# A spectral adaLN block on one core: scattered partition order of the frequencies, filter halves loaded in place, head and join reordered

## The chip, the cores and the metric

The kernel runs on one core of a Trainium2 chip. The metric is the device time of one launch in microseconds (us). Engines are named as in the profile: PE does matrix multiplications, PEld loads their weights, DVE and ACT do elementwise work and read PSUM, POOL does elementwise work in SBUF, and SP issues most transfers.

## The reference

One adaLN block on x of 2048 rows by 640 columns, in bfloat16. The rows are normalised, scaled and shifted by a modulation of `c`, filtered in the frequency domain by a complex filter W of 2048 by 321, and added back with a gate; then follow a second normalisation and a gated MLP of width 1728.

```python
sa, ca, ga, sb, cb, gb = six parts of silu(c) @ w_mod
h = _layernorm(x) * (1 + ca) + sa
x = x + ga * irfft2(rfft2(h) * (w_r + 1j * w_i))
h = _layernorm(x) * (1 + cb) + sb
x = x + gb * ((silu(h @ w_gate) * (h @ w_up)) @ w_down)
```

## The kernel before, in words

The whole schedule is written out by hand: the order of the calls in the source is the order of the instructions on each engine, and each SP transfer waits for the landing of the SP or ACT transfer eight places earlier, as the built program has it.

**Head (to about 35 us).** The row index of x is split as 1024 h + 8 p + t. For each of eight t, `st_a` (L368) multiplies two normalised tiles with a table of cosines and sines over the partitions and leaves 127 frequencies kap = p + 1 on the partitions, and one column for the two special rows; `ht_ev` (L371) copies that out, `st_b` (L377, L379) transforms the 640 columns with `Rs`, the table `Rp` scaled by 1 + ca, and `a_ev` (L383) writes A. Statistics of the rows come from `bn` on DVE (L328, L329) or `act_stats` on ACT (L333, L334), the power from POOL (L343), and `xhat` (L353 on DVE, L355 on POOL) normalises. `idle_pe` (L310) and `idle2` (L361) are matrix multiplications on a tile of ones whose results nobody reads.

**The filter.** `Wt` holds, for every partition (a frequency kap up to 128), 16 blocks of 321 columns of W: blocks 0 to 7 are rows kap + 256 k, blocks 8 to 15 are rows 255 - p + 256 k, that is, in falling order over the partitions. The first half is loaded directly (`load_w`, L284); the second is copied from DRAM to DRAM in reversed order (`flip`, L280) and then read back (L477). `wsum` (L388) adds the imaginary and the real part into a third plane.

**Join (35 to 66 us).** A is transposed so that a column l lies on the partitions of its 128 entries: `t2_dma` (L511) does four groups of columns by DMA transposes, `t2_pe` (L533) the first ones on PE. Then, for 21 groups g of up to four columns: `mix` (L552) on PE, `prod` (L576) on DVE multiplying with Wt, `stage_b` (L583), a copy on ACT (L586), `stage_c` (L608) and a copy (L617) into Em and Er. The special rows have a path of their own: `sp_w` (L406, L408) prepares their filter, `sp_sa` and `sp_sums` (L393, L415) their shift, `sp_gather` (L626) collects them from all four transposes on POOL, and `sp_mm` (L635, L640, L644) and `sp_ev` (L654, L659, L662) treat them at the groups of `SPG`; two small transfers (L663, L664) put them into row 127 of Em and Er. `ga_mod` (L669) and `mod_col` (L565) compute parts of the modulation from parts of w_mod (L478, L524, L525).

**After that.** A loop over 16 tiles (L1217 to L1222) makes x1, and the MLP (L924 to L1149) follows. Their weights are issued on SP behind the join's transfers (L766 to L778).

Of the kernel before, what the change touches and what calls it, by code (L numbers as in the profile page):

```python
# [87 lines left out]
def _tables():  # L88
# [12 lines left out]
    kap = p + 1  # L101
    M = np.zeros((P, 8, 2, 2, 128))
    H = np.zeros((128, 8, 2, P))
    for t in range(8):
        a = 2.0 * np.pi * ((kap[None, :] * (8 * p[:, None] + t)) % S) / S
        for h in range(2):
            b = 2.0 * np.pi * ((kap[None, :] * (1024 * h + 8 * p[:, None] + t)) % S) / S
            M[:, t, h, 0], M[:, t, h, 1] = np.cos(b), -np.sin(b)
        M[:, t, :, 0, 127], M[:, t, :, 1, 127] = 1.0, ((-1.0) ** p)[:, None]
        H[:, t, 0], H[:, t, 1] = np.cos(a.T), np.sin(a.T)  # L110
        H[127, t, 0], H[127, t, 1] = 1.0, (-1.0) ** p
# [9 lines left out]
    T["Ks"] = np.concatenate([K[:, 1], np.where((p % 2 == 0) & (p < 127), -1.0, 1.0)[:, None], np.zeros((128, 1))], 1).astype(_NPBF)  # L121
# [45 lines left out]
def adaln_block_kernel(ctx, tc, A_x, A_w_r, A_w_i, B_x, B_w_gate, B_w_up, B_w_down, c, w_mod, out):  # L167
# [37 lines left out]
    identb = const.tile([P, 128], BF16, name="identb")  # L205
    mv = const.tile([P, NT, 2], F32, name="mv")
# [32 lines left out]
    Wrev = rE.cut(18464, [2, 322], parts=16)  # L239
# [21 lines left out]

    nc.scalar.dma_start(c_row[:], c)
    wmca_v = wm_v[:, :, D:2 * D]
# [4 lines left out]
    load_x(2)  # L268
    nc.sync.dma_start(wm_ca[:, 0:3], wmca_v[:, 0:3])
    nc.sync.dma_start(wm_ca[:, 3:5], wmca_v[:, 3:5])  # L270
    load_m(1, 3)
    nc.sync.dma_start(Rp[:], R_dram)
    load_x(3)
    load_m(3, 8)

    dram = ctx.enter_context(tc.tile_pool(name="dram", bufs=1, space=bass.MemoryType.DRAM))
    Wflip = [dram.tile([P, 8, 321], BF16, name=n) for n in ("wflip_i", "wflip_r")]

    def flip(w, f):
        nc.sync.dma_start(f[:].rearrange("p k l -> k p l"),  # L280
                            bass.AP(tensor=w.tensor, offset=w.offset + 255 * 321, ap=[[256 * 321, 8], [-321, P], [1, 321]]))

    def load_w(i, w):
        nc.sync.dma_start(Wt[:, i, 0:8, :], bass.AP(tensor=w.tensor, offset=w.offset + 321, ap=[[321, P], [256 * 321, 8], [1, 321]]))  # L284
# [7 lines left out]
    for i, w in ((0, A_w_i), (1, A_w_r)):  # L292
        nc.sync.dma_start(Wrow[:, i, :], w.rearrange("(k2 k1) l -> k2 k1 l", k1=P)[:, 0, :])  # L293
    nc.sync.dma_start(Ktab[:], K_dram)

# [8 lines left out]
    nc.gpsimd.memset(SL[:], 0.0)  # L304
    nc.vector.tensor_reduce(out=mask4[:], in_=identb[:].rearrange("p (m r) -> p r m", r=4), axis=mybir.AxisListType.X, op=ALU.add)
# [19 lines left out]
    if True:  # L325
        def bn(ti):
            for k in range(2):
                nc.vector.bn_stats(bn6a[:, ti % 2, k, :], x_sb[:, ti, 320 * k:320 * k + 320])  # L328
            nc.vector.bn_aggr(mv[:, ti, :], bn6a[:, ti % 2])  # L329
# [15 lines left out]
        def xpair(lo):  # L345
            nc.vector.scalar_tensor_tensor(nmean[:, lo:lo + 2], mv[:, lo:lo + 2, 0], -1.0, rstd[:, lo:lo + 2], ALU.mult, ALU.mult)
            xhat(lo, nc.gpsimd)
            xhat(lo + 1, nc.vector if lo in (4, 6, 14) else nc.gpsimd)
# [41 lines left out]
        def sp_sa():  # L390
            mps = psum[:, 5, 448:448 + NC5]
            mod_cols(mps, wm_sa)
            nc.vector.tensor_copy(sa_col[:], mps)  # L393
# [17 lines left out]
        def sp_sums():  # L411
            sps = psum[:, 3, 384:384 + NL]
            for i in range(10):
                r, c2 = i // 2, i % 2
                nc.tensor.matmul(sps, lhsT=SL[:, r, c2, :], rhs=Rp[:, r, 81 * c2:81 * c2 + 81], start=(i == 0), stop=(i == 9))  # L415
            nc.vector.tensor_scalar_mul(SA[:], sps, 256.0)

# [3 lines left out]
        idle_pe(4)  # L421
        nc.scalar.activation(sc_f[:], cps, ACT.Silu)
        act_stats(3)
        nc.gpsimd.tensor_copy(sc_rep[:], sc_f[:].unsqueeze(2).to_broadcast([P, NC5, 128]))
        bn(0)
        bn(1)
        rstd_of(0, 2)
        nc.vector.tensor_copy(sc_col[:], sc_f[:])
        bn(2)
        xhat(0, nc.vector)  # L430
        xhat(1, nc.vector)
        act_var(3)
        rstd_of(2, 2)
        act_stats(5)
        bn(4)
        nc.vector.scalar_tensor_tensor(nmean[:, 2:4], mv[:, 2:4, 0], -1.0, rstd[:, 2:4], ALU.mult, ALU.mult)
        xhat(3, nc.gpsimd)
        xhat(2, nc.vector)
        idle_pe(3)
        idle2(9)  # L440
        st_a(0)
        ht_ev(0)
        act_var(5)
        rstd_of(4, 2)
        mps = psum[:, 3, 32:32 + 32 * NC5]
# [3 lines left out]
        nc.vector.tensor_scalar_add(one_p_ca[:], mps, 1.0)  # L449
        nc.vector.tensor_scalar_mul(sa4[:], mask4[:], one_p_ca[:, 4:5])  # L450
        nc.vector.tensor_scalar_mul(Rs[:, 1, 0, :], Rp[:, 4, :], sa4[:, 0:1])
        nc.scalar.mul(Rs[:, 0, 0, :], Rp[:, 0, :], one_p_ca[:, 0:1])
        nc.vector.tensor_scalar_mul(Rs[:, 1, 1, :], Rp[:, 4, :], sa4[:, 1:2])
        nc.vector.tensor_scalar_mul(Rs[:, 1, 2, :], Rp[:, 4, :], sa4[:, 2:3])
        nc.scalar.mul(Rs[:, 0, 1, :], Rp[:, 1, :], one_p_ca[:, 1:2])
        nc.vector.tensor_scalar_mul(Rs[:, 1, 3, :], Rp[:, 4, :], sa4[:, 3:4])
        nc.vector.tensor_scalar_mul(Rs[:, 0, 2, :], Rp[:, 2, :], one_p_ca[:, 2:3])
        nc.scalar.mul(Rs[:, 0, 3, :], Rp[:, 3, :], one_p_ca[:, 3:4])
        on_dve = {(4, 1), (5, 1), (6, 1)}
        for t in range(8):  # L460
            if t + 1 < 8:
                idle2(6 if t == 0 else 1)
# [4 lines left out]
            u = 2 * t + 6  # L467
            if u < NT:
                bn(u)
            if u - 2 < NT:  # L470
                xpair(u - 2)
            if u < NT:
                bn(u + 1)
                rstd_of(u, 2)
                if t == 0:
                    for i in range(2):
                        nc.sync.dma_start(Wt[:, 2 * i, 8:16, :], Wflip[i][:])  # L477
                    nc.sync.dma_start(wm_r[:, :, 0, :], wm_m[:, :, 0, :])  # L478
            if t == 6:
                nc.gpsimd.dma_start(wm_sa[:], wm_v[:, :, 0:D])  # L480
                nc.gpsimd.tensor_copy(Wrev[:, :, 0:321], _rev(Wrow, 320, [[321, 2], [-1, 321]]))
            if t == 7:
                sp_w()
# [8 lines left out]
            if t == 6:  # L492
                wsum(48, 64, 0, nc.vector)
# [10 lines left out]
    if True:  # L504
# [41 lines left out]
        def mix(g):  # L546
            ls = groups[g]
            n = len(ls)
            xps = banks(6 if g == 2 else 2 + 2 * (g % 2), 2, [4, 256])
            for i, l in enumerate(ls):  # L550
                B2, j = B2of[l][0:2]
                nc.tensor.matmul(xps[:, i, 0:192], lhsT=B2[:, j, :], rhs=KS2, start=True, stop=True)  # L552
                if i == 0:
                    for c5 in {NG - 3: (0, 1), NG - 2: range(NC5), NG - 1: (2, 3, 4)}.get(g, ()):
                        mod_col(psum[:, 2 + 2 * (g % 2), 192 + c5:193 + c5], wm_r[:, :, 1 + g % 2], c5)
# [22 lines left out]
        def stage_b(g, PP):  # L578
            n = len(groups[g])
            yps = banks((g + 1) % 2, 1, [4, 128])  # L580
            for ps in (1, 0):
                for i in range(n):
                    nc.tensor.matmul(yps[:, i, :], lhsT=_rev(PP, 64 * n * ps + i, [[n, 128]]), rhs=identb[:],  # L583
# [40 lines left out]
        def sp_gather():  # L624
            for B2, n, ls in spec:
                nc.gpsimd.tensor_tensor(B2sp[:, ls], B2[:, 0:n, 127], SA[:, ls], ALU.add)  # L626
# [4 lines left out]
        def sp_mm(i, g):  # L631
            b = 2 + 2 * (g % 2)
            if i == 0:
# [16 lines left out]
        def sp_ev(i, g):  # L650
            b = 2 + 2 * (g % 2)
            if i == 0:
# [47 lines left out]
        SPG = (10, 12, 14)  # L700
# [3 lines left out]
        xps0 = mix(0)  # L704
        prod(0, xps0, 0)
        prod(0, xps0, 1)
        t2_pe(2)
        xps1 = mix(1)
        prod(1, xps1, 0)
        prod(1, xps1, 1)  # L710
# [13 lines left out]
        wsum(0, 16, 8, nc.vector)  # L724
# [630 lines left out]
```

## Time and profile before

| What | Value |
|---|---|
| Runs | 253.07, 254.86, 255.16 us; median 254.86 |
| Profiled execution | 253.12 us, span 251.3 us |
| Granted TensorE clock | 0.999 |
| DVE and ACT busy | 81% and 66% of the span |
| Transfers | 32.50 MB, HBM read 24.80 MB, written 3.94 MB |
| First x tile's statistics | 3.03 us |
| Last `st_b` ends | 34.54 us |
| First `prod` | 37.45 us |
| First s1em (end of the join) | 66.19 us |

The span runs from the first instruction to the last; the time of the execution has 1.8 us more around it. A row of a timeline gives start, duration, engine, line, operation, result and operands, and in brackets how long the engine stood idle before it and what it then waited for. A row of the windows gives the time of the stretch, busy time of each engine in it, granted clock, mean share of the 16 DMA engines in use and what they moved in GB/s. SPq is SP's queue of transfer issues.

### The profile page before, as it was taken

How to read it: one execution, taken by the hardware profiler on the slowest of the kernel's cores; microseconds unless marked ns; L12 is line 12 of the kernel's file. 1: busy time of each engine (PE TensorE's matmuls, PEld its weight loads, DVE VectorE, ACT ScalarE, POOL GpSimd, SP SyncE). 2: the span in 40 equal slices, each digit the busy share in tenths (PEclk: the TensorE clock that was granted, in tenths of full speed). 3: DMA queues.
4: the chain of work that ended last, by engine and by line, in shares of the span. 5: the costliest groups of instructions: out<-in, count | busy, mean ns of one | idle time of the engine just before them, and what ended most of it. 6: DMA issues, size and time to landing. Idle time of an engine off the chain costs nothing.

```text
span 251.3 us, 5925 instructions
## 1 busy us (share of the span) xinstructions
PE 237.8 (95%) x2237; PEld 185.9 (74%) x2237; DVE 204.5 (81%) x497; ACT 166.5 (66%) x327; POOL 70.1 (28%) x102
## 2 busy tenths in 40 slices
PE   8598976999999999999999999999999999999994
PEld 3476755988899888778887778888775566556773
DVE  4898567996579999688999996878998788779974
ACT  2887743879789788768865388776247777774220
POOL 5348611599070715002002320000442000003410
PEclk9999999999999999999999999999999999999999
DMA  5987999999999899900002310400511000000111
GB/s 150 384 277 155 286 385 213 178 349 367 232 362 284 233 264 176 195 28 4 0 3 53 80 50 29 49 7 4 104 52 55 0 0 0 4 0 1 55 52 52
DMA packets 42766, 32.50 MB, mean 129 GB/s; under 512 B 21473, under 2 KB 39378, under 8 KB 42738
## 3 DMA queue, kind: packets, MB, share of 16 engines
q1 hardware_dynamic: 40976, 26.99, 41.4%
q0 software_dynamic: 1616, 5.10, 8.5%
q8 instruction: 17, 0.28, 0.5%
q14 instruction: 11, 0.09, 0.1%
q10 hardware_dynamic: 146, 0.04, 0.1%
HBM read 24.80 MB, written 3.94 MB: 114 GB/s over the span
## 4 chain that ended last, share of the span: by engine, by line
PE 77%; DMA 11%; SPq 9%; ACT 1%; issue 1%; DVE 0%; DVEq 0%; ACTq 0%
PE psum L1076 36%; PE psum L947 19%; DMA rM<-in_w_mod_dram 8%; PE psum L1046 6%; PE psum L924 3%; SPq L284 3%; PE psum L685 3%; DMA rE<-tab_M 3%; SPq L280 2%; PE psum L1217 2%; PE psum L1220 2%; PE psum L1034 2%; PE psum L583 1%; SPq L293 1%; PE psum L608 1%; PE psum L565 1%
## 5 line engine op out<-in xcount | busy, mean ns | idle before, releaser
L1076 PEld LDWEIGHTS <-rW 128*128 128x128 bf16 (+1 forms) x429 | 41.9, 98 | 12.7
L1076 PE MATMUL psum<-rW 128*128 128x256 bf16 (+1 forms) x247 | 42.2, 287 | 0.0
L973 POOL TENSOR_TENSOR rM<-rM,rL 128x320 f32<-128x320 f32 x6 | 5.4, 906 | 96.7 <-ACT rL L972 96.7
L947 PEld LDWEIGHTS <-rE 128*128 128x128 f16 (+1 forms) x196 | 19.0, 97 | 7.8
L576 DVE TENSOR_TENSOR rM<-psum,rW 128x384 bf16<-128x384 f32 (+2 forms) x42 | 20.4, 543 | 3.3 <-PE psum L552 1.9
L947 PE MATMUL psum<-rE 128*128 128x320 f16 (+1 forms) x147 | 22.9, 299 | 0.0
L1107 ACT COPY rH<-psum 128x384 f32<-128x384 f32 (+2 forms) x27 | 13.9, 517 | 7.3 <-PE psum L1076 5.6
L1076 PEld LDWEIGHTS <-rE 128*128 128x128 f16 x156 | 15.3, 98 | 4.8
L1114 ACT COPY rX<-psum 128x384 f32<-128x384 f32 (+2 forms) x27 | 14.0, 519 | 7.1 <-PE psum L1076 6.9
L1111 DVE TENSOR_TENSOR rH<-psum,rM 128x512 bf16<-128x512 f32 (+1 forms) x24 | 15.0, 623 | 4.4 <-PE psum L1076 2.6
L1130 ACT ACTIVATE rL<-psum 128x384 bf16<-128x384 f32 (+2 forms) x27 | 14.4, 532 | 5.6 <-PE psum L1076 3.4
L1115 DVE TENSOR_TENSOR rX<-psum,rX 128x384 f32<-128x384 f32 (+2 forms) x27 | 16.3, 603 | 1.9 <-ACT rX L1114 1.6
L1222 DVE SCALAR_TENSOR_TENSOR rM<-psum,rX 128x640 f32<-128x640 f32 x16 | 13.0, 820 | 4.3 <-ACT rL L689 2.9
L1101 ACT COPY rM<-psum 128x384 f32<-128x384 f32 (+2 forms) x27 | 13.9, 515 | 4.0 <-PE psum L1076 3.9
L1076 PE MATMUL psum<-rW,rE 128*128 128x256 bf16 (+1 forms) x78 | 15.6, 290 | 0.0
L1076 PE MATMUL psum<-rE,rY 128*128 128x256 f16 (+1 forms) x78 | 15.6, 290 | 0.0
L1131 ACT ACTIVATE rL<-rX 128x384 bf16<-128x384 f32 (+2 forms) x27 | 15.1, 558 | 0.0
L328 DVE BATCH_NORM_STATS2 bn6a<-rX 128x6 f32<-128x320 bf16 x28 | 12.3, 479 | 3.0 <-DMA rX<-in_A_x_dram 3.0
L1046 PE MATMUL psum<-rW 128*128 128x256 bf16 x130 | 14.5, 273 | 0.0
L586 ACT CAST rY<-psum 128x512 bf16<-128x512 f32 (+2 forms) x21 | 12.0, 579 | 3.2 <-PE psum L583 2.9
L916 DVE TENSOR_TENSOR rA<-psum,rM 128x320 bf16<-128x320 f32 (+1 forms) x27 | 12.1, 470 | 2.4 <-PE psum L924 2.3
L1046 PEld LDWEIGHTS <-rW 128*128 128x128 bf16 x130 | 12.7, 98 | 1.6
(230 smaller groups left out, 624.8 us busy)
## 6 DMA issues: line engine op xcount, KB each, us to landing
out_dram<-rA SPq DMA_DIRECT2D x31, 80.0 KB, 1.6
rX<-in_A_x_dram SPq DMA_DIRECT2D x7, 320.0 KB, 7.3
rA<-in_B_w_down_dram SPq DMA_DIRECT2D x2, 960.0 KB, 15.3
rY<-in_B_w_gate_dram POOLq DMA_DIRECT2D x2, 832.0 KB, 7.7
rM<-in_w_mod_dram SPq DMA_DIRECT2D x2, 800.0 KB, 11.2
rM<-in_w_mod_dram SPq DMA_DIRECT2D x1, 1600.0 KB
rW<-in_B_w_gate_dram SPq DMA_DIRECT2D x1, 1440.0 KB, 10.0
rW<-in_B_w_up_dram SPq DMA_DIRECT2D x2, 640.0 KB, 7.2
```

Of the source, the lines that this page charges most:

```text
L576: nc.vector.tensor_tensor(PPs[g][:, v0:v1, hl], xv[:, v0:v1, hl], in1, ALU.mult)
L947: nc.tensor.matmul(o, lhsT=lhs[rows(k), k], rhs=rhs[rows(k), k], start=start and k == ks[0], stop=stop and k == ks[-1], skip_group_check=True)
L1046: nc.tensor.matmul(gu[u], lhsT=Wgu[:, u, c5, ff * 128:(ff + 1) * 128], rhs=h2T[:, :, c5, :], start=(c5 == 0), stop=(c5 == NC5 - 1))
L1076: nc.tensor.matmul(o[:, f], lhsT=w, rhs=b, start=(start and f == 0 and i == 0), stop=(stop and f == len(groups[g]) - 1 and i == len(ops) - ...
L1101: nc.scalar.copy(c0, X)
L1107: nc.scalar.copy(c2, X)
L1111: nc.vector.tensor_tensor(c11, Z, c0, ALU.add)
L1114: nc.scalar.copy(c3, X)
L1115: nc.vector.tensor_tensor(c22, Y, c3, ALU.add)
L1130: nc.scalar.activation(g21, X, ACT.Silu, scale=-1.0)
L1131: nc.scalar.activation(g22, c22, ACT.Silu, scale=-1.0)
L1222: nc.vector.scalar_tensor_tensor(x1[:, t, :].rearrange("p (m r) -> p m r", r=4), ops.rearrange("p r m -> p m r"), 1.0, x_sb[:, t, :].rearr ...
```

## The change

The frequencies get another order over the partitions: kap = 16 (p // 16) + 16 - p % 16, falling within each block of 16 partitions and rising from block to block, with the special column at partition 112. With it both halves of Wt can be read with plain steps: the upper one with eight transfers per plane (all partitions, one block each), the lower one with eight per plane (16 partitions, eight blocks each). A permuted identity, identx, swaps partitions 112 and 127 in `stage_b`, so that the special row is at 127 again behind it. Beside this, orders change:

- wm_ca's load goes ahead of the third pair of x tiles; Rp is split over ACT's queue and SP's; the w_mod part for ga and the one for sa (`wm_sa`, before on POOL's queue) are issued on SP, the first between the two halves of the filter, the second behind them.
- Statistics of tile 1 go from DVE to ACT, those of tile 5 from ACT to DVE; the scaling of Rs goes to ACT and POOL; `xhat` of the odd tiles goes to DVE; fillers change.
- `sp_w` goes behind the last `st_b`; the sums of the filter for columns 48 to 63 (first half) and 0 to 15 go to POOL; `sp_sums` becomes `sp_mm(3)` at g 5, the other three steps go from g 10, 12, 14 to 9, 11, 13; the w_mod product for sa goes into `mix(3)`; both ga_mod go ahead of `mix(2)`.
- The transfers of row 127 into Em and Er go from POOL's queue to SP's.

```diff
-    kap = p + 1
+    kap = 16 * (np.arange(P) // 16) + 16 - np.arange(P) % 16
+    kin = kap.copy()
+    kap[112] = 113
...
+    def load_up(i, w):
+        for j in range(8):
+            nc.sync.dma_start(Wt[:, 2 * i, j, :], bass.AP(tensor=w.tensor, offset=w.offset + (16 + 256 * j) * 321,
+                                                         ap=[[16 * 321, 8], [-321, 16], [1, 321]]))
+
+    def load_down(i, w):
+        for a in range(8):
+            nc.sync.dma_start(Wt[16 * a:16 * a + 16, 2 * i, 8:16, :],
+                              bass.AP(tensor=w.tensor, offset=w.offset + (240 - 16 * a) * 321,
+                                      ap=[[321, 16], [256 * 321, 8], [1, 321]]))
...
     load_m(0, 1)
     load_x(1)
-    load_x(2)
     nc.sync.dma_start(wm_ca[:, 0:3], wmca_v[:, 0:3])
     nc.sync.dma_start(wm_ca[:, 3:5], wmca_v[:, 3:5])
+    load_x(2)
...
-    flip(A_w_i, Wflip[0])
-    flip(A_w_r, Wflip[1])
-    load_w(0, A_w_i)
-    load_w(2, A_w_r)
+    for i, w in WI:
+        load_up(i, w)
...
     nc.sync.dma_start(Ktab[:], K_dram)
+    nc.sync.dma_start(wm_r[:, :, 0, :], wm_m[:, :, 0, :])
+    for i, w in WI:
+        load_down(i, w)
+    nc.sync.dma_start(wm_sa[:], wm_v[:, :, 0:D])
...
+    for lo, hi, o in ((0, 112, 0), (112, 113, 15), (113, 127, 0), (127, 128, -15)):
+        nc.gpsimd.tensor_copy(identx[:, lo:hi], identb[:, lo + o:hi + o])
...
+        def bn(ti, n=1, mid=None):
+            for i in range(ti, ti + n):
+                for k in range(2):
+                    nc.vector.bn_stats(bn6a[:, i % 2, k, :], x_sb[:, i, 320 * k:320 * k + 320])
+                if i == ti and mid == 4:
+                    xhat(4, nc.vector)
+                    xhat(5, nc.vector)
+                elif i == ti and mid is not None:
+                    xpair(mid)
+            for i in range(ti, ti + n):
+                nc.vector.bn_aggr(mv[:, i, :], bn6a[:, i % 2])
...
-                if t == 0:
-                    for i in range(2):
-                        nc.sync.dma_start(Wt[:, 2 * i, 8:16, :], Wflip[i][:])
-                    nc.sync.dma_start(wm_r[:, :, 0, :], wm_m[:, :, 0, :])
...
             if t == 6:
-                nc.gpsimd.dma_start(wm_sa[:], wm_v[:, :, 0:D])
-                nc.gpsimd.tensor_copy(Wrev[:, :, 0:321], _rev(Wrow, 320, [[321, 2], [-1, 321]]))
+                wsum(48, 64, 0, nc.gpsimd)
+                wsum(0, 16, 0, nc.gpsimd)
...
-                nc.gpsimd.dma_start(Em[127:128].rearrange("p v q c -> p (v q c)").rearrange("p (a n) -> p a n", n=64), Osp[:, 0:64].unsqueeze(1))
-                nc.gpsimd.dma_start(Er[127:128].rearrange("p v q c j -> p (v q c j)"), Osp[:, 64:80])
+                nc.sync.dma_start(Em[127:128].rearrange("p v q c -> p (v q c)").rearrange("p (a n) -> p a n", n=64), Osp[:, 0:64].unsqueeze(1))
+                nc.sync.dma_start(Er[127:128].rearrange("p v q c j -> p (v q c j)"), Osp[:, 64:80])
...
-        SPG = (10, 12, 14)
+        SPG = (9, 11, 13, 5)
...
         t2_pe(3)
-        xps2 = mix(2)
-        ga_mod(320, 3)
-        prod(2, xps2, 0)
-        prod(2, xps2, 1)
-        sp_sa()
-        stage_a(3)
-        ga_mod(0, 3)
-        for lo, hi in ((0, 16),):
-            wsum(lo, hi, 0, nc.vector)
+        ga_mod(320, 6)
+        ga_mod(0, 7)
+        stage_a(2)
...
         for g in range(NG + 1):
             if g == 1:
-                sp_sums()
+                stage_a(3)
+                sp_sa()
```

More of the change, by code (lines that the diff above doesn't have):

```diff
@@ L205, in adaln_block_kernel @@
     identb = const.tile([P, 128], BF16, name="identb")
+    identx = const.tile([P, 128], BF16, name="identx")
     mv = const.tile([P, NT, 2], F32, name="mv")
@@ L238, in adaln_block_kernel @@
     wm_sa = rE.cut(34560, [NC5, D])
-    Wrev = rE.cut(18464, [2, 322], parts=16)
+    Wrev = rM.cut(10240, [2, 322], parts=16)
     Wsp = rE.cut(34064, [3, 2, NT, 2], parts=81)
@@ L267, in adaln_block_kernel @@
     load_x(1)
-    load_x(2)
     nc.sync.dma_start(wm_ca[:, 0:3], wmca_v[:, 0:3])
     nc.sync.dma_start(wm_ca[:, 3:5], wmca_v[:, 3:5])
+    load_x(2)
+    nc.sync.dma_start(Rp[:, 0:4], R_dram[:, 0:4])
     load_m(1, 3)
-    nc.sync.dma_start(Rp[:], R_dram)
     load_x(3)
     load_m(3, 8)
[L276 to L284, printed above, removed]
     load_x(4, 4)
-    flip(A_w_i, Wflip[0])
-    flip(A_w_r, Wflip[1])
-    load_w(0, A_w_i)
-    load_w(2, A_w_r)
+    for i, w in WI:
+        load_up(i, w)
+    for i, w in WI:
+        nc.sync.dma_start(Wrow[:, i, :], w.rearrange("(k2 k1) l -> k2 k1 l", k1=P)[:, 0, :])
     wm_m = wm_v[:, :, 2 * D:6 * D].rearrange("p k (i d) -> p k i d", i=4)
-    for i, w in ((0, A_w_i), (1, A_w_r)):
-        nc.sync.dma_start(Wrow[:, i, :], w.rearrange("(k2 k1) l -> k2 k1 l", k1=P)[:, 0, :])
     nc.sync.dma_start(Ktab[:], K_dram)
+    nc.sync.dma_start(wm_r[:, :, 0, :], wm_m[:, :, 0, :])
+    for i, w in WI:
+        load_down(i, w)
+    nc.sync.dma_start(wm_sa[:], wm_v[:, :, 0:D])
     nc.vector.memset(ones[:], 1.0)
@@ L390, in sp_sa @@
         def sp_sa():
-            mps = psum[:, 5, 448:448 + NC5]
-            mod_cols(mps, wm_sa)
-            nc.vector.tensor_copy(sa_col[:], mps)
+            nc.vector.tensor_copy(sa_col[:], psum[:, 5, 448:448 + NC5])
             nc.gpsimd.tensor_scalar_mul(sa4[:], mask4[:], sa_col[:, 4:5])
@@ L409, in sp_w @@
             nc.gpsimd.tensor_tensor(Wsp[:, 1], Wsp[:, 0], Wsp[:, 2], ALU.add)
[L411 to L416, printed above, removed]
         cps = psum[:, 3, 0:NC5]
@@ L420, in adaln_block_kernel @@
             nc.tensor.matmul(cps[:, k:k + 1], lhsT=c_row[0:1, k * 128:(k + 1) * 128], rhs=one11[:], start=True, stop=True)
-        idle_pe(4)
+        idle_pe(7)
+        idle_pe(6, 2)
         nc.scalar.activation(sc_f[:], cps, ACT.Silu)
-        act_stats(3)
-        nc.gpsimd.tensor_copy(sc_rep[:], sc_f[:].unsqueeze(2).to_broadcast([P, NC5, 128]))
+        act_stats(1)
         bn(0)
-        bn(1)
+        act_var(1)
         rstd_of(0, 2)
         nc.vector.tensor_copy(sc_col[:], sc_f[:])
+        act_stats(3)
         bn(2)
@@ L431, in adaln_block_kernel @@
         xhat(1, nc.vector)
+        for r in range(4):
+            nc.scalar.mul(Rs[:, 1, r, :], Rp[:, 4, :], mask4[:, r:r + 1])
+        mps = psum[:, 3, 32:32 + 32 * NC5]
+        st_a(0)
+        ht_ev(0)
         act_var(3)
         rstd_of(2, 2)
[L434 to L445, printed above, removed]
+        xpair(2)
+        bn(4, 2)
+        idle_pe(4, 2)
         mod_cols(mps, wm_ca, range(0, 3), 32)
@@ L448, in adaln_block_kernel @@
         mps = mps.rearrange("p (c w) -> p c w", w=32)[:, :, 0]
[L449 to L458, printed above, removed]
+        nc.scalar.activation(one_p_ca[:], mps, ACT.Identity, bias=1.0)
+        nc.gpsimd.tensor_scalar(Rs[:, 1], Rs[:, 1], one_p_ca[:, 4:5], 1.0, ALU.mult, ALU.mult)
+        rstd_of(4, 2)
+        for r in range(4):
+            nc.scalar.mul(Rs[:, 0, r, :], Rp[:, r, :], one_p_ca[:, r:r + 1])
         on_dve = {(4, 1), (5, 1), (6, 1)}
@@ L461, in adaln_block_kernel @@
             if t + 1 < 8:
-                idle2(6 if t == 0 else 1)
+                if t:
+                    idle2(1)
                 st_a(t + 1)
@@ L467, in adaln_block_kernel @@
             u = 2 * t + 6
+            if u == NT:
+                xpair(NT - 2)
             if u < NT:
[L469 to L473, printed above, removed]
+                bn(u, 2, u - 2)
                 rstd_of(u, 2)
-                if t == 0:
-                    for i in range(2):
-                        nc.sync.dma_start(Wt[:, 2 * i, 8:16, :], Wflip[i][:])
-                    nc.sync.dma_start(wm_r[:, :, 0, :], wm_m[:, :, 0, :])
+            if t == 5:
+                nc.gpsimd.tensor_copy(Wrev[:, :, 0:321], _rev(Wrow, 320, [[321, 2], [-1, 321]]))
             if t == 6:
-                nc.gpsimd.dma_start(wm_sa[:], wm_v[:, :, 0:D])
-                nc.gpsimd.tensor_copy(Wrev[:, :, 0:321], _rev(Wrow, 320, [[321, 2], [-1, 321]]))
+                wsum(48, 64, 0, nc.gpsimd)
+                wsum(0, 16, 0, nc.gpsimd)
             if t == 7:
-                sp_w()
+                nc.gpsimd.tensor_copy(sc_rep[:], sc_f[:].unsqueeze(2).to_broadcast([P, NC5, 128]))
             for ck in range(2):
@@ L491, in adaln_block_kernel @@
                     a_ev(t, ck)
-            if t == 6:
-                wsum(48, 64, 0, nc.vector)
+        sp_w()
         for ls in (slice(0, 48), slice(64, 81)):
@@ L552, in mix @@
                 nc.tensor.matmul(xps[:, i, 0:192], lhsT=B2[:, j, :], rhs=KS2, start=True, stop=True)
+                if g == 3 and i == 3:
+                    mod_cols(psum[:, 5, 448:448 + NC5], wm_sa)
                 if i == 0:
@@ L632, in sp_mm @@
             b = 2 + 2 * (g % 2)
-            if i == 0:
+            if i == 3:
+                for h in range(2):
+                    for j in range(10):
+                        o = 81 * (j % 2) + 41 * h
+                        nc.tensor.matmul(gap(128, h, 41 - h, b), lhsT=SL[:, j // 2, j % 2, :], rhs=Rp[:, j // 2, o:o + 41 - h],
+                                         start=(j == 0), stop=(j == 9))
+            elif i == 0:
                 for v in range(3):
@@ L651, in sp_ev @@
             b = 2 + 2 * (g % 2)
-            if i == 0:
+            if i == 3:
+                for h in range(2):
+                    nc.vector.tensor_scalar_mul(SA[:, 41 * h:81 - 40 * (1 - h)], gap(128, h, 41 - h, b), 256.0)
+            elif i == 0:
                 for v in range(3):
```

33 lines of the change are left out of this document (14 added, 19 removed).

## The prediction

> **What bounds the kernel now.** I read the busy shares first, then the chain of waits, then, for the stretch that the change touches (the first 60 us), each engine's timeline, the table by windows and the transfers' own queue. The page says that PE is the bound over the whole span:
>
> ```profile
> PE 237.8 (95%) x2237; PEld 185.9 (74%) x2237; DVE 204.5 (81%) x497; ACT 166.5 (66%) x327; POOL 70.1 (28%) x102
> ```
>
> That is an average. PE idles 13.5 us (251.3 less 237.8), and part of its busy time in the head is filler on `ones`. The chain of waits in order of time shows what decides between 11 and 62 us, and it is transfers, not PE:
>
> ```profile
> 11.75 5.44 SPq L280
> 17.24 4.68 SPq L284
> 21.97 2.73 SPq L284
> ...
> 29.49 10.33 DMA rM<-in_w_mod_dram
> 39.87 0.85 PE psum L669 x5
> ...
> 49.92 9.41 DMA rM<-in_w_mod_dram
> 59.37 0.40 PE psum L565 x10
> ```
>
> So the end hangs on the order of the transfers on SP: flips and filter loads (L280, L284), then the w_mod part that PE waits for at 39.87, then a second w_mod part at 59.37. The timelines of PE, DVE and POOL around the join show the waits themselves, in brackets:
>
> ```profile
> 39.87 0.85 PE L669 MATMUL psum<-rM,sc_rep 128*128 128x320 bf16 x5 [1.94 <-DMA rM<-in_w_mod_dram]
> 51.79 0.30 PE L635 MATMUL psum<-rE 128*81 128x64 bf16 x3 [0.27 <-POOL rE L626]
> ```
> ```profile
> 37.02 0.52 DVE L388 TENSOR_TENSOR rW<-rW 128x256 bf16<-128x256 bf16 x2 [0.90 <-DMA rW<-wflip_r]
> ```
> ```profile
> 50.76 0.98 POOL L626 TENSOR_TENSOR rE<-rM,SA 128x16 bf16<-128x16 bf16 x6 [1.99 <-DMA rM<-rA]
> ```
>
> Filter in place at 37.02; fourth DMA transpose landed at 50.76; its gather (L626) done at 51.74, and PE goes on at 51.79. Last, the windows (the last two columns are DMA share and GB/s):
>
> ```profile
> 18.00:20.00 2.00, 2.00 (x20) 1.81 (x21) 1.93 (x8) 1.73 (x3) 1.13 (x2) 1.00 0.56 138
> 20.00:22.00 2.00, 1.33 (x12) 0.93 (x10) 1.63 (x7) 1.71 (x3) 1.96 (x3) 1.00 0.57 145
> 26.00:28.00 2.00, 1.86 (x17) 1.39 (x15) 1.54 (x4) 1.20 (x2) 1.64 (x3) 1.00 1.02 231
> 38.00:40.00 2.00, 0.14 (x1) 0.11 (x2) 2.00 (x6) 0.24 (x1) 0.00 (x0) 1.00 1.23 167
> ```
>
> From 18 to 22 the flips run on about half of the DMA engines at 142 GB/s; by 26 the straight filter loads use all, at 231; at about 38 the queue turns from loads (345 GB/s in the window before) to transposes.
>
> **Head.** `bn(1)` (1.1 us of DVE) goes to ACT, which idles 3.65 us there, but `xhat(0)` stays behind `bn(2)`, which waits for its tile until 7.02: PE still starts at about 8.5, gain 0. The five DVE scalings of Rs (11.82 to 13.04) become one POOL pass over 648 columns (about 1.0 us, as L355's 0.99 for 640) and ACT's four (0.41 each); six fillers (0.81 us) before `st_a(1)` go. `st_b(0)` moves from 13.59 to about 12.8: 0.8. In the loop DVE gets one `xhat` more per step (0.36 us) and loses its waits for the power (0.26 and 0.27); PE's waits for POOL (0.52, 0.28) go. A step stays near 2.65 us, DVE's pace; I count 0.4 in all. The sp_w transposes leave the middle of the last step (31.82 to 33.24 with 0.84 of waiting): 1.4. `st_b(7)` ends near 32 instead of 34.54. The four identx copies sit in POOL's 1.29 us of idle before 5.45; Wrev, sc_rep and two filter sums (4 x 0.66) sit on POOL between 28 and 33, where it idled; uncovered they would delay sp_w by their 4 us, but only `Wrev` is ahead of it. Rp's fifth row on ACT's queue costs ACT one issue (L262's 0.53) ahead of a wait of 0.41 for `sc_f`, which nobody needs before 5.27. The fillers change in number only; the granted clock was 0.999 with PE idling 1.68 before `st_a(0)`, and it idles about as long again.
>
> **Transfers.** Removed: two flips, two loads, two reloads. Added: 32 transfers of 82 KB. In the built program each SP transfer waits for the landing of the one eight places earlier, so at most eight are in flight. The upper half's pattern leads with 8 rows like the flips' and unlike the straight load's, so I price it at the flips' 142 GB/s: 0.58 us each. It starts behind x at 16.5 as the flips did: 16.5 + 16 x 0.58 = 25.7. The first w_mod part follows, released about 24.5, landed near 29 (39.87 before). The lower half is 16 partitions per transfer, and no row shows such a shape. Lower bound: 0.36 us at 231 GB/s, below the issue pitch of 0.5 (L293's 0.41 and the gaps), so 0.5 holds. Upper bound: an eighth of the partitions at an eighth of x's 371 GB/s, 46 GB/s, 1.8 us each. I take 0.5, because the straight load is the nearest row in source, size of run and direction. The last eight are held by the w_mod landing at 29: 29.5 + 8 x 0.5, last landing near 35. wm_sa, moved from POOL (issue 1.09 us, now free) to SP, goes out at 33.5 and leaves the queue at 33.5 + 0.5 + 800 KB at 371 GB/s (2.2) = 36.2. The DMA transposes behind it then begin at 36.2 instead of 38: 1.8 earlier.
>
> [...]
>
> **Join.** Filter in place near 35 plus sums 0.45: first product at 35.5 instead of 37.45, PE ready at about 34. Gone from the stretch up to the group of lines 1 to 3 (44.70): PE's 1.94, DVE's wait for sa_col (1.20 + 0.42), four sums on DVE (1.21), now POOL's, which idled 7.70 us there. PE reaches that group at about 40.1, 4.6 earlier; the first transpose, 41.6 before, is there at 39.8. Then comes the next late thing. `sp_mm(0)` moves from g 10 to 9, and sp_mm(3) adds ten narrow matmuls (0.5): PE stands before it at 40.1 + 5.9 + 0.5, some 46.5. It needs the gather, which needs the fourth transpose: 50.76 - 1.8 + 0.98 = 49.9, against 50.58 at this place before. PE stalls 3.4 us in order, and of 4.6 only 0.7 is left, plus the waits of 0.27 and 0.17 after it: 1.2. The fourth transpose's issue took 3.56 us before, the second's and third's 1.97 and 2.50; if that stop of about 1.5 does not recur the gain is 2.7. Between 1.2 and 2.7 I take 2.0. The w_mod part of 59.37 follows in the same queue, shifts alike, and stays just ahead of PE.
>
> **SP behind the new wait.** The Em and Er rows move from POOL to SP, which stands before them until ACT's copies at g 13 (about 53.5) with w_down, Wp13 and the gate and up loads behind it (51.0 before). Covered: the two w_mod parts fill the engines until about 58. Uncovered it would cost the 2.5 us of lateness; those loads have slack, SP idling from 69.5 to 76. The rows land well before s1em, and POOL loses two issues (0.67 + 0.55) ahead of its RI products. 0.
>
> **Sum.** 253.12 (span 251.3 + 1.8 outside) - 2.0 = 251.1. The profiled execution lies 1.7 below the median of the runs shown and level with the lowest (253.07). I add 0.7: 251.8.
>
> **Rivals.**
> (1) The fourth transpose comes early enough and PE is not held at g 9: 4.6 less 0.5 leaves 4.1, near 249.7. For it: its slow issue looks singular. Against: even 1.5 earlier it is 1.9 us late.
> (2) The bounce goes but nothing arrives earlier, the lower half running at the flips' 142 GB/s: 27.8 + 16 x 0.58 = 37.1, wm_sa until 39.3, transposes 1.3 later than now; gather +1.3, less the 0.4 of waits and part of the slow issue: near 254. For it: small transfers at half share are what this trace shows. Against: engines are not halved here.
> (3) Slower: writing to 16 partitions at a time throttles the lower half. At 94 GB/s, midway between 142 and 46, each takes 0.87: 27.8 + 13.9 = 41.7, wm_sa until 43.9, transposes 5.9 later, the first product at 43.4; with 0.4 of waits gone and the slow issue half gone, about +5: 258. It decides from 0.57 us each. For it: x over all 128 partitions reaches 371 with every engine busy, so a partition may take only its share. Against: no row shows a limit by partition.
> [...]
>
> **How the numbers follow.** Forecast 0.45 (249.5 to 253.5 by itself: 1.2 or 2.7, with or without the offset), (1) 0.15, (2) 0.16, (3) 0.24. The range 249.0 to 258.5 leaves out most of what is beyond 258 (0.12, the 1.8 us bound of 46 GB/s with it) and the end below 249 (0.06). One per cent, about what a measurement of this kernel can tell from no change, is 2.5 us: faster is half of the forecast and (1), 0.37; the same is the other half and (2), 0.38; slower is (3) and a little of the rest, 0.25.
>
> **What would show it.** Right: first product near 35.5; no wait at the first ga_mod; a PE wait of 2 to 3.5 us at sp_mm(0), released by POOL's gather; windows 17 to 25 at half DMA share. Wrong: windows from 28 to 41 at about 100 GB/s and the first product after 40 (rival 3); no wait at sp_mm(0) (rival 1); the first `st_b` no earlier than 13.5, which takes 0.8 from the head but nothing from the sum, as the transfers set the end.

## The result and the profile after

The changed kernel takes 256.11 us (median of 13 runs, 254.59 to 257.58), the kernel before 253.94 (13 runs): a ratio of 1.0071, 95% interval 1.0046 to 1.0096. The change costs 0.7%. Ratios, here and below, count undisturbed (fast) executions of both kernels alone, so they can differ a little from the quotient of the medians. The profiled execution took 255.85 us with a span of 254.1 (before 253.12 and 251.3), at a granted clock of 0.98 (before 0.999).

The page first: PE's busy share and the second row, the granted clock in 40 slices, which was 9 throughout before.

```profile
PE 239.2 (94%) x2242; PEld 187.8 (74%) x2242; DVE 202.7 (80%) x488; ACT 168.2 (66%) x333; POOL 70.6 (28%) x106
...
PEclk9799996799999999999999999999999999999999
```

Two dips: at 6 to 13 us and at 38 to 51. The chain of waits, in order of time, consists of transfers up to 41 us and again from 49 to 62. The upper half's issues (L267, nine of them at 0.60) have taken the place of the flips, the lower half's landings that of the reloads:

```profile
23.74 0.60 SPq L267
...
27.32 5.97 DMA rW<-in_A_w_i_dram
33.31 1.69 SPq L272
36.94 3.92 DMA rW<-in_A_w_r_dram
...
48.68 0.59 ACT rY L583
49.28 0.52 SPq L506
...
52.60 9.50 DMA rM<-in_w_mod_dram
```

Between them, from 41.25 to 49.27, it runs over the first products on DVE, PE and ACT. The profile infers that ACT's copy (L583) released the issue of the fourth transpose (L506); the experiment e11_ga below bears on that.

The windows of this stretch (last three columns: granted clock, DMA share, GB/s) show the upper half (22 to 24), the w_mod part (28 to 30), the lower half (30 to 38, with a pause from 34 to 36) and the halved clock afterwards:

```profile
22.00:24.00 2.00, 2.00 (x21) 1.80 (x20) 1.94 (x8) 1.80 (x3) 1.27 (x2) 1.00 0.45 123
...
28.00:30.00 2.00, 1.86 (x20) 1.54 (x18) 1.17 (x4) 1.53 (x2) 1.64 (x3) 1.00 1.04 372
30.00:32.00 2.00, 2.00 (x22) 1.71 (x19) 0.66 (x2) 1.43 (x3) 2.00 (x4) 1.00 1.21 156
...
34.00:36.00 2.00, 1.63 (x24) 1.17 (x23) 1.45 (x6) 0.90 (x3) 0.30 (x1) 1.00 0.71 108
36.00:38.00 2.00, 2.00 (x24) 1.66 (x22) 0.00 (x0) 1.70 (x3) 0.00 (x0) 1.00 0.86 164
...
42.00:44.00 2.00, 0.76 (x6) 0.71 (x6) 2.00 (x5) 0.00 (x0) 1.22 (x4) 0.50 1.30 254
```

The pair of columns to read is share and rate. The w_mod part fills the engines and moves 372 GB/s; the lower half fills them as well (1.21) and moves 156. A row of W is 321 bf16 elements, 642 bytes; an engine then spends 1.21 x 16 x 642 / 156 = 80 ns on a row of the lower half, against 0.45 x 16 x 642 / 123 = 38 ns on one of the upper half. Engines that are busy all the time and move half as much are held up by something. In the upper half the pace is that of the issues: SP needs 0.64 us from one issue to the next (0.60 and the gap), which allows 82 KB / 0.64 us = 128 GB/s, and 123 were moved. The timelines of DVE and PE show who waits for the lower half:

```profile
41.25 1.02 DVE L404 TENSOR_TENSOR rW<-rW 128x256 bf16<-128x256 bf16 x2 [5.68 <-DMA rW<-in_A_w_r_dram]
```
```profile
9.29 2.35 PE L384 MATMUL psum<-rE 128*128 128x256 bf16 x10 [2.24 <-DVE rE L369]
...
43.24 0.80 PE L547 MATMUL psum<-Ktab,rM 128*128 128x192 bf16 x4 [5.03 <-DVE rM L573]
...
62.14 0.40 PE L562 MATMUL psum<-sc_col,rM 128*128 128x1 bf16 x10 [0.40 <-DMA rM<-in_w_mod_dram]
```

The filter is summed at 41.25 (before 37.02), PE idles 5.03 us, and the product with the w_mod part that is issued behind the transposes, at 59.37 before, starts at 62.14. These 2.77 us are the whole loss of the profiled execution (254.1 - 251.3 = 2.8). That is no accident of two runs: in the profiled executions of all twelve experiments below, the span less the start of that product lies between 191.1 and 193.3 us (before 191.9, after 192.0). So what happens ahead of it decides, to within these 2 us.

### The profile page after: what moved, and what is told of

It is laid out like the page before. It is cut to its first block, busy times and chain, and to the rows that moved or that the text cites. A ratio compares the mean times of both kernels' runs of the same rounds, so it can differ in the third digit from the quotient of the medians.

```text
span 254.1 us, 5973 instructions
## 1 busy us (share of the span) xinstructions
PE 239.2 (94%) x2242; PEld 187.8 (74%) x2242; DVE 202.7 (80%) x488; ACT 168.2 (66%) x333; POOL 70.6 (28%) x106
## 4 chain that ended last, share of the span: by engine, by line
PE 72%; DMA 16%; SPq 7%; issue 1%; DVE 1%; POOL 1%; ACT 0%; DVEq 0%; POOLq 0%
PE psum L1073 35%; PE psum L944 18%; DMA rX<-in_A_x_dram 6%; PE psum L1043 6%; DMA rM<-in_w_mod_dram 4%; PE psum L921 3%; DMA rW<-rL 3%; DMA rW<-in_A_w_i_dram 2%; SPq L267 2%; PE psum L580 2%; SPq L272 2%; PE psum L1031 2%; DMA rW<-in_A_w_r_dram 2%; PE psum L691 1%; PE psum L547 1%
## 5 line engine op out<-in xcount | busy, mean ns | idle before, releaser
L583 ACT CAST rY<-psum 128x512 bf16<-128x512 f32 (+2 forms) x21 | 11.8, 579 | 10.9 <-PE psum L580 10.7
L384 PE MATMUL psum<-rE 128*128 128x256 bf16 x80 | 11.2, 288 | 3.7 <-DVE rE L369 2.2
```

## The experiments

Theory A: the lower half, written into 16 partitions at a time, holds the engines, and all that is queued behind it on SP comes later. The rivals: the Em and Er rows that hold SP (B), PE's clock (C), two kinds of transfer that merely queue (D), the number of transfers or the rows in HBM (E). Every ratio below is against the kernel before, run beside it; the changed kernel's is 1.0071. The versions e2_blocks, e4_straight and e7_parts leave out what makes half of the filter right: e2 and e4 read the upper half's rows a second time, e7 the lower half's rows in rising order. Only their time is read.

**A straight lower half (e4_straight).**

```diff
-        for a in range(8):
-            nc.sync.dma_start(Wt[16 * a:16 * a + 16, 2 * i, 8:16, :], ...)
+        nc.sync.dma_start(Wt[:, 2 * i, 8:16, :],
+                          bass.AP(tensor=w.tensor, offset=w.offset + 321, ap=[[321, P], [256 * 321, 8], [1, 321]]))
```

> The changed kernel, with the lower half loaded by two straight transfers (128 partitions first, 656 KB each) in place of sixteen; it takes the rows in the order of the kernel before, so that half of the filter is not the reference's, and only the time is read. Theory A with the forecast's later steps: 231 GB/s, 5.7 us in all, in place near 35, first product near 35.5 to 36.5, then a PE wait of 2 to 3.5 us at the first special product for the gather behind the fourth transpose; time 250.5 to 252.5 (ratio 0.986 to 0.994). Rival B (the Em and Er rows on SP set the end): time near 256 still, with a wait for a load between 60 and 90.

Measured: 251.07 us, ratio 0.9887 (0.9844 to 0.9931). The same window and the waits of PE:

```profile
30.00:32.00 2.00, 1.66 (x17) 1.12 (x16) 1.43 (x2) 1.07 (x4) 1.92 (x4) 1.00 1.13 323
```
```profile
48.56 0.30 PE L636 MATMUL psum<-rE 128*81 128x64 bf16 x3 [1.36 <-POOL rE L621]
57.67 0.40 PE L560 MATMUL psum<-sc_col,rM 128*128 128x1 bf16 x10 [1.38 <-DMA rM<-in_w_mod_dram]
```

Same bytes, the engines as full (a share of 1.13 for 1.21), 323 GB/s: 1.13 x 16 x 642 / 323 = 36 ns a row. The first transpose was issued at 33.83 instead of 37.97, and the queue turned to the transposes at about 36 instead of 42. PE now stands at the first special product for POOL's gather, as forecast, though for 1.36 us and not 2 to 3.5. Rival B does not set the end: the rows held SP here too. That other rows are read is not the reason either: e8_turn loads the lower half's own rows straight, and its windows from 16 to 20 show 326 and 316 GB/s.

**All 128 partitions, half of the engines (e2_blocks).** `load_down` with the upper half's pattern, `ap=[[16 * 321, 8], [-321, 16], [1, 321]]`.

> The changed kernel, with the lower half loaded by the pattern of the upper half (eight rows of blocks first, 128 partitions per transfer, same bytes and count); it takes the upper half's rows, so that half of the filter is not the reference's, and only the time is read. Theory A (16 partitions per transfer throttle it): 0.62 us each like the upper half instead of about 0.78, DMA share halved, last landing near 38.5 instead of 40.9, time 1 to 2 lower than the changed kernel's 256.1 (ratio 0.999 to 1.003). If the number of engines mattered more than the partitions written, 8 instead of 16 engines would make it later than 40.9 and the time over 257.

Measured: 255.85 us, ratio 1.0089 (1.0055 to 1.0124). A miss in time, but the window is clear:

```profile
32.00:34.00 2.00, 1.85 (x24) 1.28 (x21) 1.07 (x5) 1.09 (x4) 0.81 (x2) 1.00 0.53 159
```

A row takes 0.53 x 16 x 642 / 159 = 34 ns, so the writes are not held up any more, on half of the engines. Half of the engines at 34 ns a row carry what all carry at 80: 159 against 156 GB/s. The filter was summed 1.4 us earlier (39.89), the transposes went out 0.5 earlier (37.44), and of that no gain can be measured.

**32 and 64 partitions at a time (e7_parts).**

```diff
+        n = (32, 64)[i]
+        for a in range(128 // n):
+            nc.sync.dma_start(Wt[n * a:n * a + n, 2 * i, 8:16, :],
+                              bass.AP(tensor=w.tensor, offset=w.offset + (256 - n - n * a) * 321,
+                                      ap=[[321, n], [256 * 321, 8], [1, 321]]))
```

> The changed kernel, with the lower half of the first filter in four transfers of 32 partitions (164 KB each) and of the second in two of 64 partitions (329 KB each), 16 engines each as before; rows run upward through a whole block, so that half of the filter is not the reference's, and only the time is read. Theory A (it is the partitions written at a time that throttle): 32 partitions carry about twice the rate of 16, so 0.33 to 0.40 us per 82 KB, and packets near 40 ns instead of 75; filter in place near 36, time 251 to 253 (ratio 0.99 to 0.998). [...] Rival E (it is the count of small transfers, or the HBM rows, not the partitions): same 130 GB/s, time near 256.

Measured: 255.9 us, ratio 1.0125 (1.0079 to 1.0172). The first window holds the first filter (32 partitions), the second the other (64):

```profile
30.00:32.00 2.00, 1.67 (x17) 1.12 (x16) 1.43 (x2) 1.07 (x3) 1.92 (x4) 1.00 1.18 156
...
34.00:36.00 2.00, 1.94 (x23) 1.56 (x23) 0.24 (x2) 1.36 (x3) 0.00 (x0) 1.00 1.18 169
```

Theory A's dose was wrong: 32 partitions are no better than 16, and 64 hardly better than 32 (1.18 x 16 x 642 over the rate: 78 and 72 ns a row); only 128 double the rate (e4). The number of transfers is not it either: six large ones cost what sixteen small ones cost, so E falls. What separates slow from fast here is whether one transfer covers all 128 partitions (34 ns a row in e2, 36 in e4). An early issue did not help: the first transpose was issued at 33.92, as early as in e4, but the w_mod part queued ahead of it was still moving at 40, and the fourth left SP at 50.88 (49.80 in the changed kernel). Within e7 the rate is not even. From 29 to 41, in slices of 0.3 us:

```profile
GB/s 393 346 349 163 152 161 139 146 156 186 195 186 152 146 143 169 175 203 222 137 137 143 161 190 186 156 156 156 160 166 156 198 303 341 329 350 361 303 278 100
```

From 29.9 to 38.0 it lies between 137 and 175 GB/s but for three rises: 186 to 195 from 31.7, 203 and 222 from 34.1, 190 and 186 from 35.9. Counted in bytes, each rise begins within 0.3 us of a place where the queue passes from the partitions 0..63 to 64..127, or back (329, 657 and 986 KB, near 32.0, 34.0 and 35.9), so that rows for both halves can be under way. Where it passes from 0..31 to 32..63, or from 64..95 to 96..127 (near 30.9 and 32.9), none follows. That transfers for the two halves hold each other up less than transfers for the same half is the author's reading; why it should be so was not shown.

**Upper and lower half in turn (e1_interleave).** `load_up(i, w, j)` and `load_down(i, w, j)` one after the other, rows ahead of them, Ktab and w_mod behind.

> The changed kernel, with the 16 transfers of the upper half and the 16 of the lower half issued in turn (one of each), the two row loads ahead of them, Ktab and the first w_mod part behind them. Theory A (the lower half is slow because each of its transfers writes into only 16 partitions, and the upper half because it runs on half of the DMA engines): a pair in turn lets the idle engines work on the lower half while the others carry the upper, near 0.9 us a pair instead of 0.64 + 0.78: both halves in place near 33 to 35 instead of 40.9, first product near 36 to 37 instead of 42.2, time 251 to 253 (ratio 0.99 to 1.00). Rival B (the filter's lateness is not what sets the end; the Em and Er rows holding SP until 60.6, or PE's clock, do): the first product moves but the time stays near 256 (ratio 1.005 or more). Rival D (the two kinds simply queue behind each other): 32 transfers still take 22 us, nothing moves.

Measured: 259.17 us, ratio 1.0199 (1.0146 to 1.0253). The idle engines were not filled:

```profile
26.00:28.00 2.00, 2.00 (x21) 1.58 (x19) 1.18 (x4) 1.21 (x2) 1.64 (x3) 1.00 0.72 104
```

The stretch from 18 to 38 runs at 102 to 151 GB/s, and the filter is no earlier (41.52), with w_mod now behind it. As rival D said, nothing was gained, but its reason is not shown: the two issues of a pair take SP 0.62 and 0.45 us, 1.17 with the gaps (19.63 to 20.80), and 164 KB / 1.17 us is 141 GB/s at most. A queue that is issued so slowly cannot tell whether the engines could have worked on both kinds at once.

**Fillers in PE's gap (e3_fill).** Twenty `matmul`s on `ones` ahead of `stage_a(2)`.

> The changed kernel, with 20 filler matmuls of 512 columns (0.216 us each at full clock) in PE's idle stretch ahead of the third group's mixing at 43.24. Rival C (PE's 5.03 us of idling drops the granted clock to 0.50 from 42 to 47, and that loss of some 2 us is what made the kernel slower): clock 1.00 there, the first group of lines 1 to 3 near 46 instead of 47.8, time 254 (ratio 1.000). Theory A (the same late transfers also hold SP, so that the transposes and the w_mod part behind them land at 62.1 whatever PE does): the clock rises, PE comes up to 2 us earlier to the w_mod wait, and stands there 2 us longer instead of 0.40: time at most 0.4 lower, 255.7 to 256.1 (ratio 1.005 to 1.007).

Measured: 255.53 us, ratio 1.009 (1.0055 to 1.0125). The clock was 1.00 from 42 to 44 instead of 0.50, though it fell to 0.82 and 0.50 in the two windows from 44 to 48; PE reached the w_mod product no earlier:

```profile
62.34 0.40 PE L562 MATMUL psum<-sc_col,rM 128*128 128x1 bf16 x10 [0.35 <-DMA rM<-in_w_mod_dram]
```

About half of the lost clock came back and no time with it: this speaks against rival C, though the other half stayed lost.

**The first w_mod part behind the lower half (e11_ga).** The line of that load and `ga_mod` moved behind `load_down` and `stage_a(2)`.

> The changed kernel, with the first w_mod part (800 KB) issued behind the lower half instead of ahead of it, and PE's two products with it moved behind the third group's mixing. What is queued ahead of the transposes is the same, so they and the last w_mod parts keep their place, but the filter is in place 2.2 us earlier (38.7 instead of 40.9). If the order on SP's queue (transposes, then the w_mod part waited for at 62.1) sets the end by itself: time 255.5 to 256.5 (ratio 1.006 to 1.010), PE waiting some 2 us at that part instead of 0.4. If the first product's lateness sets it: 253.5 to 254.5 (ratio 0.999 to 1.003).

Measured: 256.37 us, ratio 1.0093 (1.0064 to 1.0122).

```profile
40.11 0.80 PE L547 MATMUL psum<-Ktab,rM 128*128 128x192 bf16 x4 [4.65 <-DVE rM L573]
62.02 0.40 PE L562 MATMUL psum<-sc_col,rM 128*128 128x1 bf16 x10 [1.14 <-DMA rM<-in_w_mod_dram]
```

The filter was summed 3.1 us earlier (38.12) and PE resumed 3.1 earlier (40.11 for 43.24), and all of it was gone at 62.02. Two of these 3.1 us went on PE itself: the ga_mod products, moved behind the third group's mixing, took 2.87 us there, and the first product on DMA-transposed columns started at 46.63 instead of 47.79. Most of the rest went into the wait for w_mod, 1.14 instead of 0.40. ACT's copy that the profile named as the releaser of the fourth transpose ended 1.2 us earlier (48.10 for 49.27), yet that transpose left SP no earlier (50.01 for 49.80), which speaks against the copy holding it. What stayed the same is the queue ahead of the transposes: 800 KB, the lower half, 800 KB, in another order.

**Rows from POOL's queue again (e6_rows).** `nc.gpsimd.dma_start` for the Em and Er rows.

> The changed kernel, with the Em and Er rows written from POOL's queue again, so that SP no longer stands from 53.6 to 60.6 with the down, gate and up weights behind it. Theory A: these loads had slack, the time stays within 0.5 of the changed kernel's (ratio 1.004 to 1.009). Rival B (the 10 us by which w_down is held decide): time falls by 1.5 or more (ratio 1.002 or less).

Measured: 256.58 us, ratio 1.0129 (1.0104 to 1.0155): w_down went out at 55.90 instead of 61.86, and nothing was gained. Rival B falls.

**The loads of before in the changed order (e5_bounce).** Tables, `flip`, `load_w` and reloads of the kernel before; head, loop, join and the other queues as changed.

> The changed kernel with one part undone: the partition order and the loads of the filter are those of the kernel before (two flips into DRAM, two straight loads, two reloads), the order of head, loop and join and the queue of wm_sa, Em and Er stay as changed. Theory A (the loss comes from the lower half's transfers alone): filter in place near 37 again instead of 40.9, transposes begin near 38 or a little earlier, the first w_mod part is waited for at its landing near 40, and the reordered join gives back a little: time 252.5 to 254.5 (ratio 0.995 to 1.003). Rival B (the reordered join or the rows on SP cost time by themselves): time stays over 255 (ratio 1.005 or more).

Measured: 253.49 us, ratio 0.9999 (0.9973 to 1.0026). The whole loss sits in the filter's loads (with the partition order that goes with them). The reordered head and join give nothing by themselves while the loads are as long as before: PE then waits 1.85 us for w_mod and 1.70 for the gather, where e4 shows what they give when the data are early.

**A version without either (e8_turn).** Both halves straight; the lower half turned around by PE with a reversed identity.

```diff
+                    nc.tensor.matmul(ps[:, 256 * h:256 * h + 256] if n > 1 else ps, lhsT=identr[:],
+                                     rhs=_rev(Ws, 8 * 321 * i + lo + 160 * h, dims[1:] if n > 1 else dims), start=True, stop=True)
...
+                        engs[i](_rev(Wt, 2 * WP * i + 8 * 321 + lo, dims), pv)
```

> A version built on theory A: partition order of the kernel before, both halves of the filter loaded straight (128 partitions first, four transfers of 656 KB), the lower half into a spare place, and turned around there by PE with a reversed identity (some 22 matmuls of 256 columns, about 2.5 us) and copied to its place by ACT and DVE (twelve copies, about 7 us, the first pair ahead of the first product, the last three pairs during the join); the rest as changed. Theory A: transposes begin near 34, the w_mod part lands near 57.7, first product near 36.5 to 37; time 250.5 to 252.5 (ratio 0.987 to 0.996). If ACT or DVE in the join becomes the bound through the copies: 253 to 255.

Measured: 252.89 us, ratio 0.9977 (0.9953 to 1.0001). The queue was empty from 32 to 36, but the copies in the join held DVE's products:

```profile
43.97 1.02 DVE L586 TENSOR_TENSOR rM<-psum,rW 128x384 bf16<-128x384 f32 x2 [2.89 <-PE psum L324]
...
46.29 2.62 DVE L586 TENSOR_TENSOR rM<-psum,rW 128x192 bf16<-128x192 f32 x6 [1.22 <-ACT rW L412]
```

**Turned in the loop, two pieces a step (e9_early), and w_mod ahead of the transposes (e10_early_wmod).** Quarter pieces in the two halves of one bank.

> The turning version again, with the turning and its copies taken out of the join: fourteen of twenty quarter pieces (256 columns each) are turned in the loop's steps 3 to 7, six copied by ACT in steps 3 to 5, six by DVE in steps 5 to 7, two by ACT in the last step, the rest ahead of the first product. In the version before it three pairs of copies stood between the first products (ACT's copy held 1.04 us by DVE's products, DVE's products 2.89 and 1.22 us by ACT and PE). Theory A (the join is served by data that are early, and nothing but the order of the copies cost the gain): first product near 37, no DVE wait over 0.6 up to 48, PE held at the first special product for the gather near 49; time 250 to 251.5 (ratio 0.984 to 0.992). If the copies only move the loss into the loop (DVE and ACT are busy there): 252 to 253.5.

> As e9_early, with the last two w_mod parts (2.4 MB) issued ahead of the DMA transposes, in the stretch from 30 to 35 us in which the queue had nothing to carry (0 to 41 GB/s in the turning version), and four more fillers ahead of the first step against the halved clock of the head. Theory A: the w_mod part is in place long before 57, SP is free 1 us earlier behind the transposes, the transposes begin no later than 36.5; time as e9_early or up to 1.4 lower, 249 to 251 (ratio 0.980 to 0.990). Against: 2.4 MB need 6.5 us at 371 GB/s, up to 37, and hold the transposes and with them the gather and the first special product by 1 to 2 us: then 1 higher than e9_early.

Measured: ratio 1.0242 (1.0196 to 1.0288) and 1.0275 (1.0221 to 1.0328). Both missed: the second piece, in the same bank, waited for the copy of the first, and PE stood for 0.51 to 1.60 us in each of these steps (e9, in an execution of 263.93 us).

```profile
24.72 0.28 PE L421 MATMUL psum<-rW,identr 128*128 128x256 bf16 x1 [1.54 <-ACT rW L422]
```

**One bank, one copy (e12_banks).**

> The turning version (straight loads, lower half turned around by PE) with what its early variant got wrong taken back: there the two quarter pieces of a step lay in one bank of PSUM, and PE stood 1.54 us in each step for the copy of the first before it wrote the second. Here a step turns one pair of pieces at a time (512 columns, one bank, one copy): seven of ten pairs in steps 3 to 7 of the loop (ACT copies in 3 to 5, DVE in 6 and 7, ACT the last), three and the middle column ahead of the first product, none in the join; the w_mod part of 1.6 MB that PE waits for near 62 goes out ahead of the DMA transposes, in the stretch from 30 to 35 in which the queue carried nothing; four more fillers in the head. Theory A: loop steps 2.65 to 2.9 us, no wait for ACT or DVE over 0.6 at the turning, first product near 37.5, transposes begin near 35, no wait for w_mod near 57 to 60; time 249.5 to 251.5 (ratio 0.982 to 0.991). If the copies do not fit beside the loop's own: steps of 3 us or more from the third on, 253 or more.

Measured: 252.04 us, ratio 0.9954 (0.9923 to 0.9984): 0.5% faster than the kernel before, where the changed one is 0.7% slower. It differs from e8 and e9 in several things at once (which copies stand where, w_mod ahead of the transposes, fillers), so no share of the gain is put down to one of them. No wait for w_mod is left at its product (57.89). A step that waits 1.46 us for DVE's copy at 31.87 and transposes that are issued from 36.98 instead of 35 are what its trace has beyond the expectation of 251.5.

## Why the prediction was wrong

**The step that failed** is the lower half: "The last eight are held by the w_mod landing at 29: 29.5 + 8 x 0.5, last landing near 35". It landed at 40.9. The larger part is the count. Seven of the sixteen transfers were issued before the w_mod part landed, but by the records of the packets all sixteen moved behind its bytes, from 29.7 on: 8.0 us at the forecast's own price instead of 4.0. Rivals 2 and 3 of the same prediction count all sixteen; the forecast did not. The other part is the price: 1.31 MB took 10.0 us, to the last row at 39.7, 0.63 us each instead of 0.5, another 2.0 us. While the queue was fed, at 156 and 164 GB/s, a transfer took 0.50 to 0.53 us, so 0.5 was right there; the rest went mostly into the pause from 34 to 36, behind the issue that took 1.69 us (33.31). The 1.2 us from the last row to the landing were allowed for (1.5, from 33.5 to 35).

The reason given for 0.5 was wrong all the same: the straight load is near in source and direction but not in the partitions that it covers (e4, e7). Its own price is 0.25 us per 82 KB (323 GB/s in e4), half the forecast's.

**What hung on it** went as the sum's own logic says. The queue was to turn to the transposes at 36.2 (38 before); it turned at about 42. First product: 35.5 forecast, 42.18 measured. In e4 these are about 36 and 36.45, but by luck of the terms: sixteen transfers' bytes at the straight price take 4.1 us, as eight at the forecast's price would. With the times thus given, the join's working can be read from e4: a gain of 2.0 was forecast, its ratio is one of 2.9. PE ready near 34 (34.37 in the changed kernel), no wait at the first ga_mod and a stall for the gather at the first special product were right. The size of that stall (1.36, about 3.4 forecast) was not, nor that w_mod stays just ahead of PE (a wait of 1.38).

**Rival 3** named the mechanism and put its threshold at 0.57 us each; 0.63 was measured. Its price was too high: 0.87 each and 258, where 256.1 came. Its reason, a share for every partition, is wrong: 64 partitions run hardly faster than 16 (169 GB/s in e7, 156 in the changed kernel).

**The head.** "PE still starts at about 8.5, gain 0": it started at 9.29, because DVE's statistics of tile 2 waited until 7.80 (7.02 before) for x tiles now queued behind wm_ca. `st_b(0)` started at 14.44, not 12.8. As the prediction said of this case, it took nothing from the sum: PE waited later anyway.

**Upper half.** Half share was right (0.45 to 0.48), though it did not set the price: 0.58 us each was 0.64, SP's issue time of 0.60 with the gap, and half of the engines could move more (159 GB/s at a share of 0.53 in e2). Its last rows moved near 26.5 instead of 25.7.

**SP behind the new wait** at cost 0: right (e6). **Fillers** at cost 0: the clock did fall, to 0.50 for about 3.4 us in the head (0.96, 0.50 and 0.69 in the windows from 8 to 14) and 6.8 in the join (0.64, 0.50, 0.50 and 0.65 from 40 to 48), which the prediction had not reckoned with; e3 speaks against the time hanging on that.

## What to carry to other kernels

Price a load by what it covers at both ends: a transfer that writes fewer than all 128 partitions, or leads with eight rows, ran at half the rate of a straight one here (156 to 169 and 159 GB/s against 323), in pieces of 82 to 329 KB, and everything later in its queue pays the difference. Write down what stands ahead of each transfer in the queue before counting how many are behind an event: here that count was the larger error. Where the order of rows has to change, a straight load and a turn on an engine with idle time (here PE with a reversed identity) can be cheaper than a clever access pattern (a ratio of 0.9954 in e12, 1.0071 in the changed kernel), if its copies do not stand between the products.

## What the runs showed of the hardware

- Rows of 642 bytes took 36 ns on an engine when a transfer covered 128 partitions and 72 to 80 ns when it covered 16, 32 or 64, with the engines full in both (shares of 1.13 in e4; 1.21 in the changed kernel, 1.18 in e7). On half of the engines they took 34 to 38 ns (shares of 0.53 in e2, 0.45 in the upper half).
- Where the queue passed between rows for partitions up to 63 and rows from 64 on, the rate of such transfers rose from between 137 and 175 GB/s to between 186 and 222, for 0.6 to 0.9 us (e7, three times).
- The granted clock is not told by the length of an idle stretch alone: in the head it halved after 1.73 us of idling in e5 (0.56 and 0.58 in the next windows) and after 2.24 in the changed kernel (0.50 and 0.69), and stayed at 1.00 after 2.71 in e2 and 2.98 in e3.
